# Attention of nine pairs in 64-token sub-chunks on 64x64 tiles, with r loaded four tokens to a partition and w spread by a product

## The chip, the cores and the metric

The kernel runs on one core of a Trainium2 chip. The metric is the device time of one execution in microseconds; the median of several runs counts. A core has a matrix engine (TensorE, PE in the profile; its weight loads are PEld), a vector engine (VectorE, DVE), a scalar engine (ScalarE, ACT), a general engine (GpSimd, POOL) and a queue engine for transfers (SyncE, SP). They run side by side, each through its own instructions in order, and wait for each other by semaphores. Sixteen DMA engines move data between the device memory and the on-chip memory of 128 partitions. TensorE writes to eight banks of 128 x 512 float32.

## The reference

Four batches, eight heads, 768 tokens, 48 channels a head. First a decaying linear attention, then a block that mixes tokens and channels:

```python
def _attn_ref(r, k, v, w, u):
    state = np.zeros((B, H, D, D))
    for t in range(S):
        kt, vt, rt = k[:, :, t], v[:, :, t], r[:, :, t]
        cur = np.einsum('bhd,bhe->bhde', u[None] * kt, vt)
        y[:, :, t] = np.einsum('bhd,bhde->bhe', rt, state + cur)
        state = w[None, :, :, None] * state + np.einsum('bhd,bhe->bhde', kt, vt)

def _moe_ref(x, w_theta, w_tok_r, w_tok_i, w_ch):   # x: y with heads side by side
    theta = x @ w_theta
    zr, zi = x * np.cos(theta), x * np.sin(theta)
    u = x + (np.einsum('ts,bsd->btd', w_tok_r, zr) + np.einsum('ts,bsd->btd', w_tok_i, zi))
    return u + np.maximum(u @ w_ch, 0.0)
```

## The kernel before

The 768 tokens of a batch are three *pairs* of 128-token chunks, so there are twelve pairs, g = 0 to 11 (g = 3b + pr). `front(b)` does attention, theta and z for the three pairs of a batch, `mixing(b)` the token and channel products. In a pair, k and r are multiplied by powers of w (`kpow`, `rpow`; tasks Kw and Rw, DVE or POOL, L539 and L541), transposed by TensorE against the identity (`flip`, L477) and copied out of the bank (L492 on ACT, L493 on DVE) to KT and RT. Then come the scores K'R (L585), their causal mask (mAT, L594, always on DVE), the diagonal with the bonus u (PD L601, diag L618, yd L627), the outer products of k and v for the state (L651), the running state (sums F and T, L695 to L703; decay N, L706; 16-bit copies Sb or Sd, L666 to L685) and the output, as states times r plus masked scores times v, gathered in two banks y.

There are two forms of a pair. In the *two-token form* (pairs 0 to 6, those in `PAIRS`) a partition holds two neighbouring tokens, k and v come in pieces of 384 bytes, scores are 64x64 tiles with 128 columns, four masks of 512 columns are made, the states' product (L727), two straight products (L740) and the bonus (L756) add up in the banks, and ACT or DVE copies x out (L764, L766). In the *chunk form* (pairs 7 to 11) k and v come in pieces of 192 bytes, scores are 64x128 tiles by rows (16 products), there are four masks too, the states take 16 products of 64 rows (L779), the masked scores times v 16 full products (L792), and DVE adds yd while it takes x out (L801). r always comes with two tokens to a partition.

x is transposed, by TensorE or by a DMA (L483), and multiplied by w_theta (L815); ACT takes cosine and sine (L822, L826), DVE makes z (L830). In `mixing`, six products of 128 tokens sum over z (`mix`, L852: for each of six output chunks three parts of four products), DVE adds x (un, L870), then comes a transpose, the product with w_ch (L884), and the last sum: DVE alone (L893), or ACT and POOL (L890, L897). The token weights are cast to 16 bits by POOL's transfers (`cast`, L446), transposed by TensorE in twelve blocks (`weights`), and used by the mixing from then on.

The powers of w: `w_row` is loaded by ACT's queue into all 128 partitions (L293), in a part of the memory of z; ACT takes its logarithm (L374) and six exponentials scaled by token counts (L381).

Nothing of the order is left to a scheduler on the chip. Each piece of work is a *task*; lists written out by hand give the order of all tasks (`ORDER`), the engine where there is a choice (`WAYS`), the bank of each use (`BANKS`), extra waits (`AFTER`) and filler products of zeros that write to an idle bank (`IDLE`, and the tasks warm0 and warm1 of six and eight products; all at L284). Each engine executes its tasks in that order and waits where an operand isn't there yet.

## Time and profile before

| | |
|---|---|
| median of 3 runs | 139.91 us (139.69 to 140.66) |
| profiled execution, first to last instruction | 138.9 us |
| PE, DVE, ACT, POOL busy | 127.6, 107.5, 76.7, 61.7 us |
| q1 (SP's and ACT's transfers): packets, share of 16 DMA engines | 64720, 75.6% |
| q0 (POOL's casting loads): packets, share | 2432, 12.4% |
| loads of k and v, chunk form | 20 of 192 KB |
| loads of k, v (two-token form) and r | 7, 7 and 12 of 384 KB |

The profile gives one time for its execution, the span, and the three times of the runs apart from it; the median of the runs is 1.0 us above the span. Busy time counts the time in which an engine has an instruction in work; for PE the ends of instructions are modelled, and neighbouring ones overlap, so that the length of one is more than its share of a row of them. Where a line lists a wait, the name behind the arrow is what ended it.

### The profile page before, as it was taken

The numbers are of one execution on the slowest core, as the hardware profiler recorded it, in microseconds if no ns is written. First come the engines' busy times: TensorE is split into PE (matmuls) and PEld (weight loads), VectorE is DVE, ScalarE is ACT, GpSimd is POOL, SyncE is SP. The second block draws the span as 40 slices with busy tenths as digits, with TensorE's granted clock in tenths as the row PEclk, the third lists the DMA queues.
The fourth block names the chain that finished last, engine by engine and source line by source line (L and its number), as shares of the span: only waits on it lengthen the run. The fifth ranks groups of instructions, "written<-read, shape, count | busy, mean of one in ns | idle before, by whom it ended". The sixth has DMA issues, their size and how long they took to land.

```text
span 138.9 us, 4469 instructions
## 1 busy us (share of the span) xinstructions
PE 127.6 (92%) x1874; PEld 85.0 (61%) x1874; DVE 107.5 (77%) x205; ACT 76.7 (55%) x145; POOL 61.7 (44%) x70
## 2 busy tenths in 40 slices
PE   0999569999996999999999999999999999999990
PEld 0334347977764767777766687577565665656640
DVE  2419397889799999999979997999699986427281
ACT  2455687799992368593898039629903133650020
POOL 5003977861041099949320199993118902002000
PEclk9999985799999999999999999999999999999999
DMA  2999999999999999739979999999972563803635
GB/s 46 250 263 263 261 225 213 210 239 211 248 254 267 261 196 147 107 67 174 193 127 267 169 217 185 147 269 187 288 177 60 103 181 87 257 0 115 114 122 218
DMA packets 67340, 25.65 MB, mean 185 GB/s; under 512 B 61816, under 2 KB 67320, under 8 KB 67320
## 3 DMA queue, kind: packets, MB, share of 16 engines
q1 hardware_dynamic: 64720, 22.22, 75.6%
q0 software_dynamic: 2432, 2.95, 12.4%
q10 hardware_dynamic: 168, 0.20, 0.7%
q8 instruction: 14, 0.23, 0.7%
q14 instruction: 6, 0.05, 0.1%
HBM read 20.25 MB, written 4.72 MB: 180 GB/s over the span
## 4 chain that ended last, share of the span: by engine, by line
PE 65%; DVE 10%; DMA 8%; POOL 6%; SPq 4%; issue 2%; ACT 2%; DVEq 0%; ACTq 0%; POOLq 0%
PE bank L852 25%; PE bank L477 9%; DMA ld<-in_v_dram 8%; PE bank L815 6%; PE bank L884 5%; PE bank L284 5%; PE bank L585 4%; POOL Kw L539 3%; PE bank L651 2%; SPq L432 2%; PE bank L740 2%; DVE Rw L539 2%; DVE PD L601 2%; PE bank L756 1%; PE bank L792 1%
## 5 line engine op out<-in xcount | busy, mean ns | idle before, releaser
L852 PE MATMUL bank<-z,WrT 128*128 128x384 bf16 x144 | 46.8, 326 | 0.0
L852 PE MATMUL bank<-z,WiT 128*128 128x384 bf16 x144 | 46.8, 326 | 0.0
L594 DVE TENSOR_TENSOR mAT<-bank,mask 128x512 bf16<-128x512 f32 x28 | 18.1, 681 | 4.3 <-PE bank L585 4.1
L539 POOL TENSOR_TENSOR Kw<-ld,kpow 128x768 bf16<-128x768 f32 x4 | 8.2, 2040 | 24.5 <-DVE Kw L539 9.9
L852 PEld LDWEIGHTS <-WrT 128*128 128x128 bf16 x144 | 14.0, 98 | 8.1
L852 PEld LDWEIGHTS <-WiT 128*128 128x128 bf16 x144 | 14.1, 98 | 8.0
L870 DVE TENSOR_TENSOR uu_all<-bank,x 128x384 bf16<-128x384 f32 x24 | 13.0, 549 | 4.9 <-PE bank L852 4.7
L826 ACT ACTIVATE trig<-bank 128x384 f16<-128x384 f32 x24 | 11.4, 504 | 7.9 <-PE bank L815 7.8
L627 POOL TENSOR_TENSOR yd<-dg,vb 128x768 bf16<-128x768 f32 x10 | 14.7, 1470 | 2.3 <-ACT lwu L403 1.3
L492 ACT ACTIVATE RT<-bank 128x1024 bf16<-128x1024 bf16 x11 | 11.3, 1026 | 6.8 <-PE bank L477 6.6
L884 PE MATMUL bank<-Wch,uu_all 128*128 128x384 bf16 x72 | 14.6, 326 | 0.1
L897 POOL TENSOR_TENSOR fin_all<-fin_all,uu_all 128x384 f32<-128x384 f32 x8 | 7.3, 913 | 16.1 <-ACT fin_all L890 14.8
L815 PE MATMUL bank<-Wth,xT 128*128 128x384 bf16 x72 | 14.3, 326 | 0.0
L284 PE MATMUL bank<-zero 128*128 128x512 bf16 x31 | 10.9, 503 | 3.6 <-DVE zero L291 3.6
L822 ACT ACTIVATE trig<-bank,pi 128x384 f16<-128x384 f32 x24 | 13.6, 594 | 0.7 <-PE bank L815 0.6
L830 DVE TENSOR_TENSOR z<-x,trig 128x1536 bf16<-128x1536 bf16 x12 | 11.7, 974 | 2.9 <-ACT trig L822 2.9
L492 ACT ACTIVATE KT<-bank 128x1024 bf16<-128x1024 bf16 x11 | 11.5, 1044 | 3.3 <-PE bank L477 3.0
L594 DVE TENSOR_TENSOR mAT<-bank,mask_c 128x512 bf16<-128x512 f32 x20 | 13.0, 681 | 0.2 <-PE bank L585 0.2
L539 POOL TENSOR_TENSOR Rw<-ld,rpow 128x768 bf16<-128x768 f32 x4 | 7.2, 1812 | 8.2 <-DVE PD L601 8.1
L893 DVE SCALAR_TENSOR_TENSOR fin_all<-bank,uu_all 128x384 f32<-128x384 f32 x16 | 8.6, 551 | 2.2 <-PE bank L884 1.8
L539 DVE TENSOR_TENSOR Rw<-ld,rpow 128x768 bf16<-128x768 f32 x8 | 9.2, 1152 | 1.0 <-DMA ld<-in_r_dram 1.0
L477 PE MATMUL bank<-ident,Kw 128*128 128x128 bf16 x96 | 7.4, 219 | 2.5 <-POOL Kw L539 2.5
(112 smaller groups left out, 219.6 us busy)
## 6 DMA issues: line engine op xcount, KB each, us to landing
ld<-in_r_dram SPq DMA_DIRECT2D x12, 384.0 KB, 6.0
out_dram<-fin_all SPq DMA_DIRECT2D x11, 384.0 KB, 3.1
ld<-in_k_dram SPq DMA_DIRECT2D x7, 384.0 KB, 10.5
ld<-in_v_dram SPq DMA_DIRECT2D x7, 384.0 KB, 6.1
ld<-in_k_dram SPq DMA_DIRECT2D x10, 192.0 KB, 4.8
ld<-in_v_dram SPq DMA_DIRECT2D x10, 192.0 KB, 5.2
z<-in_moe_w_tok_i_dram POOLq DMA_DIRECT2D x1, 384.0 KB, 7.3
fin_all<-in_moe_w_tok_r_dram POOLq DMA_DIRECT2D x1, 384.0 KB, 8.4
```

The costliest lines, as they stand in the source:

```text
L284: ins = [nc.tensor.matmul(bank_t[k][:, :wide * C].rearrange("p (a c) -> p a c", a=wide), zero, bc(zero, 1, wide), start=True, stop=True, s ...
L477: ins = [nc.tensor.matmul(bank16(tok)[:, i * C:(i + 1) * C], s, ident, is_transpose=True, start=(i == 0), stop=(i == n - 1)) for i, s in e ...
L492: ways = [act(n * C, lambda: nc.scalar.activation(dst, src(), Act.Copy)), dve(n * C, lambda: nc.vector.tensor_copy(dst, src()), 1.0 if pai ...
L539: return eng.tensor_mul(to.rearrange("p j h d -> p h j d")[:, :, :, :D], tokens(i), pw)
L594: mask01[:, j] if pairs else mask_c): nc.vector.tensor_mul(
L627: return eng.tensor_mul(yd.rearrange("p a b d -> p (a b) d"), wide(dg, D), vb.rearrange("p a b d -> p (a b) d"))
L815: ins = [nc.tensor.matmul(bank(th)[:, :HD], xT[:, t, dk, :], Wth[:, dk, :], start=(dk == 0), stop=(dk == ND - 1)) for dk in range(ND)]
L822: P.add(act(HD, lambda th=th, t=t, trig=trig: nc.scalar.activation(trig[:, t, 0], bank(th)[:, :HD], Act.Sin, bias=pi2), 144), use=[th], rd ...
L830: P.add(dve(4 * HD, lambda trig=trig, pr=pr: nc.vector.tensor_mul(z[:, 2 * pr:2 * pr + 2], bc(x[:, 2 * pr:2 * pr + 2], 2, 2), trig), 2.0, ...
L852: ins.append(nc.tensor.matmul(bank(tm)[:, :HD], (WrT, WiT)[ri][:, so, to * C:(to + 1) * C], z[:, so, ri], start=(part == 0 and i == 0), st ...
L870: P.add(dve(HD, lambda tm=tm, t=t, to=to, un=un: nc.vector.tensor_add(un[:, t], bank(tm)[:, :HD], x[:, to])), use=[tm], rd=[("x", xi, pr, ...
L884: ins = [nc.tensor.matmul(bank(tf)[:, :HD], uT[:, t, dk, :], Wch[:, dk, :], start=(dk == 0), stop=(dk == ND - 1)) for dk in range(ND)]
```

## The change

Pairs 3 to 11, nine in all, get a new form; pairs 0 to 2 keep the two-token form.

- In the new form k and v lie as in the chunk form. Each 128-token chunk is two sub-chunks of 64 tokens. The scores are 32 products of 64x64 tiles with 64 columns, only the two diagonal blocks of a chunk, so that a pair has two masks of 512 columns in place of four. The state is carried from sub-chunk to sub-chunk: three sums F (or two and a last Sb) and up to four 16-bit states in place of two. The states take 32 products in two tasks, the masked scores times v 32, the outer products 32 on 64x64 tiles. The second mask waits for the states' second task (`fence`).
- r is loaded with four neighbouring tokens of a head to a partition, in pieces of 768 bytes, by two DMAs of 64 partitions each. `rpow` has four exponentials of 192 columns, and the transposes of r give the heads in the order 0, 2, 1, 3 of the head pairs.
- w is loaded as one row; ACT takes its logarithm on one partition, TensorE multiplies it by a column of ones into two banks (`spread`), and the exponentials read the banks.
- `wu`, the small load for w and u by channel, may go by POOL's queue or SP's too; sums, casts and copies get other engines.
- Order, engines, banks, extra waits and fillers are new throughout. POOL issues the first casting load before its first Kw, four behind that Kw, one after Kw1, and the one for w_theta after Kw2; all twelve weight transposes stand before the first mixing product in PE's order. PE's order begins: spread, wu flip, K flip of pair 0, a weight flip, the eight fillers warm1, outer products of pair 0, r flip of pair 0, scores. DVE's order from the first Rw to the first z is Rw0, vb0, mask, KT copy, F, a weight copy, PD0, wup, Rw1, place, two masks, blank, uw, T, Sb, yd0, three masks, PD1, two masks, a weight copy, a mask, two weight copies, an x copy, mask_c, Sb, F, a weight copy, T, Rw3, Rw2, N, z0. The last sums are on DVE alone 21 times (16 before), on ACT and POOL 3 times (8 before).

The core of the diff:

```diff
-PAIRS = (0, 1, 2, 3, 4, 5, 6)
+PAIRS = (0, 1, 2)
...
 IDLE = [
-    (28, 0, 5), (73, 3, 5), (71, 3, 5), (83, 2, 1), (119, 0, 1),
+    (21, 2, 2), (32, 3, 3), (5, 5, 3), (91, 7, 1), (81, 7, 1), (88, 3, 2), (99, 0, 3),
+    (100, 5, 3), (44, 4, 2), (135, 1, 1), (166, 3, 2),
 ]
...
-        P.add((ACT, 2950, False, lambda: nc.scalar.dma_start(out=w_row, in_=rows_of(w, C))),
-              wr=["w_row"], prio=-3e4, name="w_row", kind="small")
+        P.add((ACT, 460, False, lambda: nc.scalar.dma_start(
+            out=w_row, in_=w.rearrange("(a h) d -> a h d", a=1))),
+              wr=["w_row"], prio=-3e4, name="w_row", kind="small", desc=(2, 1, 70))
...
+        def spread():
+            ins = [nc.tensor.matmul(bank("lw")[:, :HD], ones, w_row.rearrange(
+                "p h d -> p (h d)"), start=True, stop=True, skip_group_check=True)]
+            for hh in range(2):
+                ins.append(nc.tensor.matmul(
+                    bank("lw4")[hh * Q:(hh + 1) * Q, :HD // 2], ones[:, :Q],
+                    w_row[:, hh * HP:(hh + 1) * HP].rearrange("p h d -> p (h d)"),
+                    start=True, stop=True, skip_group_check=True))
+            return ins[0], ins[-1]
+        P.add(pe(1900, spread), rd=["lw", "ones"], acq=["lw", "lw4"], prio=-199.5, mode=5,
+              name="spread")
...
+        if what == "r":
+            for hh in range(2):
+                P.add(sp(lambda hh=hh: nc.sync.dma_start(
+                    out=Ls[i][hh * Q:(hh + 1) * Q].rearrange("p (x n) -> p x n", x=HP),
+                    in_=rows[hh * HP:(hh + 1) * HP].rearrange("x (p i) d -> p x (i d)", i=4))),
+                    wr=[("L", i, hh)], prio=-90 + 0.001 * nload[0], desc=(0, 16, 38.5),
+                    name="load r", kind="load")
...
+                def fine(tk=tk, KT=KT, RT=RT):
+                    ins = []
+                    for c in range(2):
+                        for y in range(HP):
+                            for hi, a in ((0, 0), (1, 1), (0, 1), (1, 0)):
+                                q, s = slice(hi * Dp, (hi + 1) * Dp), slice(a * Q, (a + 1) * Q)
+                                o = (c * HP + y) * Q
+                                ins.append(nc.tensor.matmul(
+                                    bank(tk[hi])[s, o:o + Q], KT[q, y, c, s], RT[q, y, c, s],
+                                    start=(c == 0 and y == 0), stop=(c == 1 and y == HP - 1),
+                                    skip_group_check=True))
+                    return ins[0], ins[-1]
...
+                        ins.append(nc.tensor.matmul(
+                            bank(ts[a])[hi * Dp:(hi + 1) * Dp, o:o + D], Kw[q, m, h, :], vm,
+                            start=first, stop=(hp == HP - 1), skip_group_check=True))
...
+            steps = [(ts[0], 0)] if pairs else [(ts[0], 0), (ts[1], 0), (ts[0], HP * D)]
+            for n, (tok, o) in enumerate(steps):
+                S, kS = new_sb(pairs)
+                Ss.append((S, kS))
...
+                add_up(F, tok, o, [kF], running)
+                to_16(S, kS, pairs, F, kF, "Sb1")
+                running = (F, kF)
...
+                def states(ty=ty, RT=RT, Ss=Ss, c=0, begun=begun):
+                    ins = []
+                    for y, hp in enumerate(at_slot):
+                        for hi, a in ((0, 0), (1, 1), (0, 1), (1, 0)):
+                            S = Ss[2 * c + a][0]
+                            if S is None:
+                                continue
+                            q, s = slice(hi * Dp, (hi + 1) * Dp), slice(a * Q, (a + 1) * Q)
+                            o = (c * HP + hp) * D
+                            ins.append(nc.tensor.matmul(
+                                bank(ty[hi])[s, o:o + D], RT[q, y, c, s], S[q, hp, :],
+                                start=(hi, a) not in begun, stop=False, skip_group_check=True))
+                            begun.add((hi, a))
+                    return ins[0], ins[-1]
...
+                masked(0)
+                masked(1, held, [("states", g)])
+
+                def intra(ty=ty, vb=vb, m=mAT2[0], off=0):
+                    m = m.rearrange("p i h t -> p i (h t)").rearrange(
+                        "p i (x t) -> p i x t", t=Q)
                     ins = []
                     for c in range(2):
                         for hp in range(HP):
-                            for hi in range(2):
...
+                            for a in range(2):
+                                s, hi = slice(a * Q, (a + 1) * Q), a ^ off
                                 o = (c * HP + hp) * D
                                 ins.append(nc.tensor.matmul(
...
+                                    bank(ty[hi])[s, o:o + D],
+                                    m[s, hi, c * HP + at_slot[hp], :],
+                                    vb[s, c, 2 * hp + hi, :], start=False,
+                                    stop=(c == 1 and hp == HP - 1), skip_group_check=True))
```

398 lines of the change are left out of this document (205 added, 193 removed), and 83 rows, old and new, of the table ORDER.

## The prediction

> **What bounds the kernel now.** I read the page's shares and slices first, then busy time by stretch, then the chain of waits, then single rows of the start. The first fence has lines of the page: span, busy share of two engines, granted TensorE clock and DMA share in 40 slices of 3.47 us.
>
> ```profile
> span 138.9 us, 4469 instructions
> PE 127.6 (92%) x1874; PEld 85.0 (61%) x1874; DVE 107.5 (77%) x205; ACT 76.7 (55%) x145; POOL 61.7 (44%) x70
> ...
> PEclk9999985799999999999999999999999999999999
> DMA  2999999999999999739979999999972563803635
> ```
>
> The second fence is the busy time of each engine by stretch; the numbers in brackets are instructions.
>
> ```profile
> 9.50:18.50 9.00, 6.44 (x82) 3.67 (x82) 6.00 (x14) 5.25 (x6) 5.94 (x5) 1.00 1.26 263
> ...
> 19.80:26.30 6.50, 6.50 (x133) 4.84 (x133) 5.49 (x11) 4.87 (x13) 4.22 (x7) 0.50 1.19 211
> ...
> 43.00:66.00 23.00, 23.00 (x530) 16.76 (x532) 22.62 (x43) 12.81 (x25) 15.04 (x17) 1.00 0.94 169
> 66.00:115.00 49.00, 48.69 (x673) 33.37 (x670) 43.99 (x77) 27.20 (x53) 25.25 (x23) 1.00 0.93 183
> 115.00:131.00 16.00, 16.00 (x100) 9.67 (x99) 6.90 (x11) 4.99 (x11) 1.82 (x2) 1.00 0.50 123
> ```
>
> From 43 us on PE is busy in all but 0.3 us of 88 us, so there the time is the sum of PE's work. DVE is nearly full beside it until 66 (22.62 of 23.00) and has room later (6.90 of 16.00). Before 43 PE is fed badly: the DMA engines are full, DVE is busy for two thirds (6.00 of 9.00) to five sixths (5.49 of 6.50) of the time, and from 19.8 to 26.3 TensorE has half its clock. So two numbers decide: when the first mixing product starts (the first work that PE has in plenty), and how much PE work is left then. The third fence has pieces of the chain in order of time (start, length, what).
>
> ```profile
> 35.50 0.65 PE bank L852 x4
> ...
> 37.57 0.68 PE bank L477 x12
> ...
> 40.37 2.50 DVE Rw L539
> 42.87 0.05 issue
> ...
> 60.16 0.34 PE bank L727 x8
> 60.50 0.50 PE bank L740 x32
> 61.00 0.34 PE bank L756 x4
> 61.35 0.57 PE bank L585 x32
> 61.92 0.76 PE bank L651 x48
> ...
> 80.86 0.55 PE bank L585 x16
> 81.42 0.32 PE bank L779 x16
> ...
> 84.69 0.40 PE bank L792 x16
> ...
> 86.18 0.24 PE bank L651 x8
> ...
> 134.58 0.68 PE bank L884 x3
> ```
>
> The first mixing product starts at 35.5, the last PE work ends at 135.3 (134.58 + 0.68): 99.8 us, in which PE once waits about 1.1 us, for the slow decay product at 40.37 that ends at 42.87. After 135.3 come 3.6 us of last output. 35.5 + 99.8 + 3.6 = 138.9, the span. The median of the runs is 139.9, so 1.0 us lies around the span; I add it at the end.
>
> **PE's work behind the first mixing product.** (a) The attention forms. A pair in the old two-token form costs, from these pieces, states 0.34, straight products 0.50, bonus 0.34, scores 0.57, outer products 32/48 of 0.76 = 0.51: 2.26 us, without transposes and the diagonal, which all forms share. A pair in the old chunk form: scores 0.55, states 0.32, products with v 0.40, outer products 2 x 0.24 = 0.48: 1.75. The new form issues four groups of 32 products on 64x64 tiles. Its groups exist in the trace only as relatives: 32 products cost 0.50 (48 columns, two row tiles), 0.51 (48 columns, four tiles) and 0.57 (128 columns, four tiles). I take 0.50 each and 0.1 more because the states are split into two tasks between other work: 2.10. Four pairs (3 to 6) leave the two-token form, 4 x -0.16 = -0.6; five (7 to 11) leave the chunk form, 5 x 0.35 = +1.75: +1.1 in all. Bounds: if a group costs two thirds of that (0.34, as 8 wide products do), 9 x -0.64 brings the +1.1 to -4.7; if 32 small products cost twice what 16 do (0.80), 9 x 1.2 brings it to +12. The three relatives lie at 0.50 to 0.57, so I stay near them. Half the masks and fewer columns go away, but not PE instructions: their number doubles against the chunk form. (b) The new order puts all twelve weight transposes ahead of the first mixing product; before, six lay behind it. 36 products at 0.68/12 = 0.057 are -2.0. (c) In return all of pair 2's attention comes behind it, 2.26 less half its outer products, which the last pair of a batch doesn't need: +2.0, and one x transpose more, +0.34. Sum: +1.1 - 2.0 + 2.0 + 0.3 = +1.4. (d) The 1.1 us wait at 42: in the new order that place looks different, and I take the wait as gone; if its like returns, that is +1.1.
>
> In a sentence by itself: the Trainium skill, "TensorEngine Tiling (Array Packing)", section Key Properties, says that a change of tiling mode drains TensorE; the new PE order changes mode 53 times where the old did 44, and this trace agrees in kind, since 16 states cost 0.32 and 32 products 0.50 with changes around them. By that rule alone the sum would be about 1 us longer, by 9 changes at an estimated 0.1 us; the split states above hold nearly all of it already.
>
> **The start.** The fourth fence has rows of the start in order of time.
>
> ```profile
> 2.45 1.28 ACT L303 ACT_TABLE_LOAD   x1 [2.45 <-issue]
> ...
> 5.55 0.52 ACT L374 ACTIVATE z<-z 128x384 f32<-128x384 f32 x1 [1.82 <-DMA z<-in_w_dram]
> ...
> 6.63 1.10 ACT L381 ACTIVATE rpow<-z,tok_f 128x384 f32<-128x384 f32 x2
> ...
> 9.85 0.96 DVE L539 TENSOR_TENSOR Rw<-ld,rpow 128x768 bf16<-128x768 f32 x1
> ```
>
> The logarithm of w waits 1.82 us for w in 128 rows. As one row it should come sooner; the bounds are the end of the table load, 3.73, and 5.55. I take 4.1, near the lower, for 1.5 KB is little. Then 0.52 for the logarithm; then the new product that spreads the row, whose price no row shows: the change plans 1.9 us for three products, the first of which is half the columns, 0.95 (from below 0.3, if it ran as the 512-column fillers do; from above 1.9). Then four full exponentials at 0.55, four half as wide at about 0.35 (192 columns) and a small one of 0.2, in ACT's queue before the last rpow: 3.8. The first r decay starts at 4.1 + 0.52 + 0.95 + 3.8 = 9.4, against 9.85: little gained, since twice as many exponentials stand in its way.
>
> From there DVE's own queue up to the first z (which releases the first mixing product) is the bound, since PE has slack there (it is given 23 filler products). The fifth fence has the groups that price it: mean ns of one stands after the comma.
>
> ```profile
> L594 DVE TENSOR_TENSOR mAT<-bank,mask 128x512 bf16<-128x512 f32 x28 | 18.1, 681 | 4.3 <-PE bank L585 4.1
> ...
> L830 DVE TENSOR_TENSOR z<-x,trig 128x1536 bf16<-128x1536 bf16 x12 | 11.7, 974 | 2.9 <-ACT trig L822 2.9
> ...
> L601 DVE TENSOR_TENSOR PD<-RT,KT 128x1024 bf16<-128x1024 bf16 x10 | 7.2, 720 | 0.3 <-ACT RT L492 0.3
> ...
> L801 DVE TENSOR_TENSOR x<-bank,yd 128x384 bf16<-128x384 f32 x10 | 5.2, 551 | 1.6 <-PE bank L792 1.5
> ...
> L493 DVE COPY WrT<-bank 128x768 bf16<-128x768 bf16 x4 | 2.2, 545 | 0.0
> ...
> L699 DVE TENSOR_TENSOR F<-bank,N 128x192 f32<-128x192 f32 x4 | 1.4, 354 | 0.3
> ```
>
> 8 masks x 0.681 = 5.4; 4 Rw x 0.95 = 3.8; 6 copies of transposes x 0.545 = 3.3; 2 PD x 0.72 = 1.4; z 0.97; five sums of 192 x 0.354 = 1.8; yd0 about 0.95 (as a decay product). That is 17.6. The K copy, v's cast, two state casts and the small constants that stand among them I estimate at 5.0 from rows of like size. 22.6 in all, plus 1.0 for the first F, which waits until PE is through eight fillers and the first outer product: 9.4 + 22.6 + 1.0 = 33.0, and 0.2 to the product. First mixing product at 33.2, against 35.5. Before, the same place was reached with four masks more done, but the half clock cost PE time there; now PE has the weight transposes to fill it, so a half clock would cost less.
>
> DVE in all: masks 18 x -0.681 = -12.3; 18 more sums x 0.354 = +6.4; five more x and five more final sums at 0.55 = +5.5; four K and four x transposes copied on DVE instead of one each, about +3.6; fewer Kw, PD, casts, about -2. Sum +1.2: DVE is not relieved, its masks are traded for work that ACT and POOL had. Behind the first mixing product its share remains as it was, so it costs nothing more than now; if its cover were gone, each us of DVE before 66 would be a us. Where the second mask waits for the states (the new fence), DVE's queue behind it waits too; this is up to 9 short waits, and I allow them to be hidden.
>
> **DMA.** The sixth fence compares loads in 0 to 12 us with 19 to 36 us, when POOL's casting loads of the weights run.
>
> ```profile
> ld<-in_r_dram SPq DMA_DIRECT2D x3, 384.0 KB, 5.9
> ```
>
> ```profile
> q0 software_dynamic: 1936, 2.51, 82.8%
> q1 hardware_dynamic: 2933, 1.11, 32.6%
> ...
> ld<-in_r_dram SPq DMA_DIRECT2D x2, 384.0 KB, 13.7
> ```
>
> While casts run (q0), SP's loads get 1.11 MB in 17 us, 65 GB/s, and land 13.7 us after issue instead of 5.9. The casts are moved forward: one ahead of POOL's first Kw, four right behind it. r in 768-byte pieces gains a little, k and v of pairs 3 to 6 in 192-byte pieces lose a little; I take these as equal, for the DMA engines are full until about 55 us (the slices) either way and the loads come in the order of their use.
>
> **The sum.** 33.2 + (99.8 - 1.1 + 1.4) + 3.6 = 136.9 for the span; the 0.2 that the fence waits may show makes it 137.1, and with the 1.0 around it 138.1 (-1.3%).
>
> **The rivals.** *Slower, starved start:* five casts before 16 us take the DMA engines for about 14 us (six took 17), in which SP gets 65 x 14 = 0.9 MB. Pair 1's second half of r must be in DVE's hands at about 15.4 (9.4 and the 6 us that stand before Rw1); all behind it, masks of pair 0 too, waits in order. If it lands at 20 the first mixing product comes at 37.8 and the time is 142.7; it is slower by over 1% from a landing at 18.6. Against it: r1 and k1 are issued early, and some will have landed before the casts start. In a sentence by itself: the Trainium skill, "DMA: Bandwidth & Descriptors", section Queues, rings and completion order, says that an engine turns between queues by whole packets, so a queue of large packets gets the larger part; the 82.8% against 32.6% above agree.
> *No change:* the small products cost 0.57 instead of 0.50 a group, or fence waits show: 9 x 0.28 = 2.5 more, 140.6.
> *More:* the groups cost 0.40 and the start holds: 9 x -0.4 = -3.6, 134.5; half of it 136.3.
>
> **How the numbers follow.** Forecast (137.0 to 139.2) 0.42; more (below 137.0) 0.20; no change by dearer products (139.2 to 141.3) 0.16; starved start (above 141.3) 0.22. One per cent, 1.4 us, is about what a measurement of this kernel can tell from no change. Faster by over 1% (below 138.5): 0.20 and 0.27 of the forecast, 0.47. Within: 0.15 + 0.16 = 0.31. Slower: 0.22. The range 135.5 to 142.6 leaves out about a tenth on each side; the forecast's own is 137.0 to 139.2.
>
> **What would show it.** Right: the first L852-like mixing product near 33, PE without gaps from about 35 on, groups of 32 products near 0.50, masks 30 instead of 48. Wrong: Rw1 on DVE waiting for a load, PE idle before 20 for longer than now, a late theta product waiting for its weight, or DVE full and PE with gaps between 40 and 110.

## The result, and the profile after

| | before | changed |
|---|---|---|
| median | 139.91 us | 155.51 us (153.76 to 155.88) |
| ratio | | 1.106 (95% interval 1.099 to 1.114) |
| span of the profiled execution | 138.9 us | 153.5 us |
| first mixing product starts | 35.34 | 39.11 |
| last PE work ends | 135.24 | 149.50 |

The change made the kernel 15.6 us slower. Medians are over all executions; the ratios, here and below, leave out those that ran in a slower state of the chip. In the prediction the first mixing product before is at 35.5, since the chain shows its second piece; it starts at 35.34. The first fence has lines of the changed kernel's page, to be laid beside those of before.

```profile
span 153.5 us, 5331 instructions
...
PE 133.3 (87%) x2286; PEld 86.8 (57%) x2286; DVE 108.4 (71%) x223; ACT 72.4 (47%) x146; POOL 58.8 (38%) x62
...
PEclk9999999999999999599999999987999999999999
DMA  1999999999999999858778999999999396611545
...
L660 DVE TENSOR_TENSOR mAT<-bank,mask_c 128x512 bf16<-128x512 f32 x18 | 11.8, 683 | 1.2 <-PE bank L856 0.7
```

PE has 2286 products in place of 1874, but is busy only 5.7 longer. The span grew by 14.6, so most of it is time in which PE did nothing. (The medians lie 15.6 apart. In nearly all executions recorded later the time is 1.7 to 1.9 above the span, so the 138.9 must belong to the slowest of the three runs before, 140.66.) Recorded half clock stood in slices 6 to 8 before, where PE had slack; now it stands in the 17th and in the 27th and 28th, where PE has none. The clock row is no witness for the start: the trace's clock records begin at 17.05 (at 9.29 before), and until then PE worked at about half its later speed, as the fillers below show. The DMA engines are full from the second slice on, as before; the hole of before in slices 17, 18 and 21 is one from 17 to 22 now. The next two fences, of before and after, give the stretch from the first mixing product to the last PE work (length, busy time of PE, PEld, DVE, ACT and POOL, granted clock, DMA share, GB/s).

```profile
35.34:135.24 99.90, 98.40 (x1395) 66.59 (x1392) 83.97 (x143) 53.08 (x103) 44.19 (x42) 1.00 0.84 172
```

```profile
39.11:149.50 110.39, 103.17 (x1871) 68.54 (x1867) 84.57 (x159) 52.47 (x110) 43.32 (x37) 0.97 0.90 155
```

The ledger of the 14.6 follows from them: 3.8 in the start (39.11 - 35.34), 4.8 more of PE's busy time (103.17 - 98.40), 5.7 more of PE's idle time (7.22 - 1.50), and 0.4 in the tail. The waits of PE in that stretch, from the view of waits, are these (what PE's line waited for: sum, times, longest):

```profile
PE bank L524 <- POOL Kw L592: 2.2, 1, 2.2
PE bank L718 <- issue: 1.9, 1, 1.9
PE bank L973 <- DMA uu_all<-uu_all: 1.5, 1, 1.5
PE bank L524 <- DVE uu_all L959: 1.1, 1, 1.1
PE bank L973 <- DVE x L891: 0.3, 1, 0.3
```

Before, that view has one line there, the 1.1 for Rw that the prediction named. The first is pair 10's K, whose load landed at 100.3; the second is a wait "for nothing that the profile shows"; the third a DMA transpose that took 4.96; the fourth a transpose of K on PE behind work of DVE, which had itself waited 1.59 and 0.41 for loads of r and k (from 85.8 on). The start is in these rows of DVE and PE:

```profile
12.40 0.96 DVE L587 TENSOR_TENSOR Rw<-ld,rpow 128x768 bf16<-128x768 f32 x1 [8.67 <-DMA ld<-in_r_dram]
...
17.85 0.36 DVE L750 COPY F<-bank 128x192 f32<-128x192 f32 x1 [2.50 <-PE bank L718]
```

```profile
12.77 4.66 PE L292 MATMUL bank<-zero 128*128 128x512 bf16 x11
17.36 0.44 PE L718 MATMUL bank<-vb,Kw 64*64 64x48 bf16 x32
...
25.42 2.10 PE L292 MATMUL bank<-zero 128*128 128x512 bf16 x9
```

The exponentials were ready at 9.35, but Rw0 waits for the second half of r until 12.40. Eleven fillers stand ahead of the outer products and take 4.66, 0.42 each, where nine of them take 2.10 later, 0.23 each; F waits for the outer products until 17.85.

### The profile page after: what moved, and what is told of

It is laid out like the page before. It is cut to its first block, busy times and chain, and to the rows that moved or that the text cites. A ratio compares the mean times of both kernels' runs of the same rounds, so it can differ in the third digit from the quotient of the medians.

```text
span 153.5 us, 5331 instructions
## 1 busy us (share of the span) xinstructions
PE 133.3 (87%) x2286; PEld 86.8 (57%) x2286; DVE 108.4 (71%) x223; ACT 72.4 (47%) x146; POOL 58.8 (38%) x62
## 3 DMA queue, kind: packets, MB, share of 16 engines
q1 hardware_dynamic: 67100, 22.23, 80.8%
## 4 chain that ended last, share of the span: by engine, by line
PE 64%; DMA 10%; DVE 7%; ACT 7%; issue 4%; POOL 3%; SPq 2%; DVEq 0%; ACTq 0%; POOLq 0%
PE bank L941 24%; PE bank L973 9%; PE bank L524 9%; DMA ld<-in_k_dram 7%; PE bank L292 6%; PE bank L905 5%; DMA uu_all<-uu_all 3%; PE bank L881 2%; PE bank L648 2%; ACT WrT L539 1%; DVE mAT L660 1%; PE bank L718 1%; PE bank L856 1%; SPq L476 1%; POOL Kw L590 1%
## 5 line engine op out<-in xcount | busy, mean ns | idle before, releaser
L973 PE MATMUL bank<-Wch,uu_all 128*128 128x384 bf16 x72 | 15.7, 350 | 1.9 <-DMA uu_all<-uu_all 1.5
L697 POOL TENSOR_TENSOR yd<-dg,vb 128x768 bf16<-128x768 f32 x10 | 14.6, 1473 | 6.3 <-DVE pi L306 5.2
L959 DVE TENSOR_TENSOR uu_all<-bank,x 128x384 bf16<-128x384 f32 x24 | 12.7, 551 | 5.5 <-PE bank L941 5.3
L982 DVE SCALAR_TENSOR_TENSOR fin_all<-bank,uu_all 128x384 f32<-128x384 f32 x21 | 11.2, 553 | 5.7 <-PE bank L973 5.7
L587 DVE TENSOR_TENSOR Rw<-ld,rpow 128x768 bf16<-128x768 f32 x8 | 7.9, 992 | 10.3 <-DMA ld<-in_r_dram 10.3
L292 PE MATMUL bank<-zero 128*128 128x512 bf16 x37 | 13.0, 481 | 0.0
L524 PE MATMUL bank<-ident,Kw 128*128 128x128 bf16 x96 | 8.1, 233 | 5.6 <-POOL Kw L590 2.3
L660 DVE TENSOR_TENSOR mAT<-bank,mask_c 128x512 bf16<-128x512 f32 x18 | 11.8, 683 | 1.2 <-PE bank L856 0.7
L524 PEld LDWEIGHTS <-Kw 128*128 128x128 bf16 x96 | 6.6, 104 | 8.3 <-POOL Kw L590 3.2
L973 PEld LDWEIGHTS <-uu_all 128*128 128x128 bf16 x72 | 6.9, 106 | 6.5 <-DMA uu_all<-uu_all 2.0
L539 ACT ACTIVATE KT<-bank 128x1024 bf16<-128x1024 bf16 x8 | 8.2, 1030 | 4.9 <-PE bank L524 4.9
L891 DVE TENSOR_TENSOR x<-bank,yd 128x384 bf16<-128x384 f32 x18 | 9.2, 550 | 0.5 <-POOL N L781 0.3
```

The costliest lines, as they stand in the source:

```text
L292: ins = [nc.tensor.matmul(bank_t[k][:, :wide * C].rearrange("p (a c) -> p a c", a=wide), zero, bc(zero, 1, wide), start=True, stop=True, s ...
L524: ins = [nc.tensor.matmul(bank16(tok)[:, i * C:(i + 1) * C], s, ident, is_transpose=True, start=(i == 0), stop=(i == n - 1)) for i, s in e ...
L539: ways = [act(n * C, lambda: nc.scalar.activation(dst, src(), Act.Copy)), dve(n * C, lambda: nc.vector.tensor_copy(dst, src()), 1.0 if pai ...
L587: return eng.tensor_mul(to.rearrange("p i x d -> p x i d")[:, :, :, :D], fours(i), pw)
L660: mask01[:, j] if pairs else mask_c): nc.vector.tensor_mul(
L697: return eng.tensor_mul(yd.rearrange("p a b d -> p (a b) d"), wide(dg, D), vb.rearrange("p a b d -> p (a b) d"))
```

## The experiments

Four theories were set against each other. (1) The new order costs: late loads, products and fillers ahead of pair 0, stores and transposes ahead of loads in SP's queue. (2) The new form of nine pairs costs. (3) The new load formats slow the DMA. (4) PE waits for its own instructions. All edits are to the changed kernel's lists, unless said otherwise; in diffs a line gives an engine's order. There r0a and r0b are the two halves of pair 0's load of r (k and v alike), wu is the small load of w and u, `cast Wi2` a casting load and `flip Wi5` a transpose on PE of a token weight's block, TU a transpose of an output block by DMA, `out` an output store, and a number behind "fillers" their count. The first four runs have line numbers 7 lower than the changed kernel.

**The start, step by step.**

```diff
-SP: wu w, r0b, k0, v0, r0a, ...
+SP: r0b, r0a, k0, wu w, v0, ...          (first run)
-POOL: cast Wi2, Kw0, cast Wi1, ...
+POOL: Kw0, cast Wi2, cast Wi1, ...       (second run, with the first)
-WARM = [6, 8]; 3 fillers behind warm1
+WARM = [6, 1]; none behind warm1         (third run, with both)
```

> Changed kernel; in SP's order the loads of r (pair 0, both halves) and of k (pair 0) come before the small load of w by channel. Nothing else is moved. Changed kernel: median 155.5, Rw0 begins at 12.40 after a wait for r's second half, first mixing product at 39.23. If the late first loads set the start (theory 1): Rw0 begins at 10.0 to 11.0, the first mixing product comes 1 to 2.4 earlier, total 153.0 to 154.5. If the new form of nine pairs is what costs (theory 2): no gain beyond 0.5. If DMA as a whole is slower by the new formats (theory 3): r's loads get shorter waits only as far as others get longer ones, total within 0.5 of 155.5.

> As the run before, and the first casting load, of a token weight, is issued behind Kw0 instead of before it on POOL. Theory 1 (the casting load takes DMA share from r, k and v of pair 0): Rw0 begins at 9.4 to 10.0, which is when the last of its exponentials is there, first mixing product at 36 to 37.5, total 152 to 153.5. Theory 2: no gain. If the casting load doesn't matter: the same as the run before within 0.3.

> As the run before, and ten of the eleven filler products ahead of pair 0's outer products are left out (warm1 one product in place of eight, the three behind the weight flip gone). Theory 1: the outer products begin when Kw0 and vb0 are there, so F of pair 0 comes 2 to 3 earlier than in the run before, but the granted clock may stay at 0.5 longer; first mixing product 1 to 3 earlier than in the run before if the clock doesn't matter, equal or later if the fillers had bought the clock. Theory 2: no gain.

Measured: 154.32, 155.59 and 154.57; first mixing product at 40.3, 42.8 and 41.1. In the first Rw0 came at 11.82, as the late load of w now held up ACT's exponentials. Rw0 did come at 9.4 in the second and third, just as the prediction had it, and nothing was won: PE's fourth task is the flip of a weight block, and it now waited for its casting load. This is PE in the second run:

```profile
9.16 1.03 PE L517 MATMUL bank<-ident,Kw 128*128 128x128 bf16 x8 [0.18 <-POOL Kw L583]
16.81 0.39 PE L517 MATMUL bank<-ident,z 128*128 128x128 bf16 x2 [6.62 <-DMA z<-in_moe_w_tok_i_dram]
```

Between the first and the second run only that casting load was moved, and Rw0 came 2.4 earlier (9.40 for 11.82): the casting load had held up the loads beside it. With it moved, the weight came late in its place. All of theory 1's numbers for the first mixing product were missed; its total for the first run (153.0 to 154.5) was met, but with a later start, so not for its reason.

**The new form in the old order.**

```diff
-order of the changed kernel
+order of the kernel before, mapped task by task; PAIRS = (0, 1, 2)
```

> The new form of nine pairs, with all loads in their new formats and the spread of w, but tasks in the order of the kernel before: its order on all engines, the masked scores of a new-form pair held back by three PE tasks behind its states, no extra waits by hand, five groups of fillers as before. Only where the new form uses more banks at a time are some tasks of pairs 9 and 10 later. Theory 1 (the new order and its queues cost, the form doesn't): first mixing product at 33 to 36, total 138 to 143. Theory 2 (the form costs): first mixing product as in the kernel before, total 150 or more, the difference spread over pairs 3 to 11. Theory 3 (the load formats cost): loads of k and v land late, PE waits on Kw and Kw's DMA from pair 5 on, total 147 or more.

Measured: 156.51, ratio 1.114 (1.104 to 1.124), first mixing product at 37.5. This hits theory 2's number, but not its reason: PE had gaps of 10.9 behind the first mixing product. Of these, 4.4 lay between 114 and 120, where PE's outer products and others waited for DVE's sums F and T; whether a lack of banks was behind that is tested in the fourteenth run, below.

**Start and loads.** The fifth run also moves what stood ahead of pair 0 on PE and DVE. The sixth changes SP's order in the middle only, and the eighth does both.

```diff
-PE: wuflip, flip K0, flip Wi5, warm1 x8 +3, outer0, flip R0, scores0.1, flip K1, scores0.0, flip Wi2
+PE: wuflip, warm1 x3, flip K0, flip R0, outer0, scores0.1, flip K1, scores0.0, flip Wi5, flip Wi2
-SP: v6a, out2, k7b, k7a, out1, r9a, TU0, k9b, r9b, k9a, v7b, out0, ...
+SP: v6a, k7b, k7a, k9b, k9a, r9a, r9b, out2, out1, TU0, v7b, k10b, k10a, out0, ...
```

> Changed kernel with four edits to the start, nothing else: r and k of pair 0 first in SP's order and the first casting load behind Kw0 (as in the second run); warm1 three products in place of eight and ahead of pair 0's K flip, the three more fillers behind it gone; r's flip ahead of the outer products; the flip and the copy of the first weight block, for which PE waited 6.0 in the second run, moved behind the scores on PE and behind the masks on DVE. Theory 1 (the start is lost by the order of DMAs, and by products that stand ahead of pair 0 in PE's order): Rw0 at 9.4, F of pair 0 at about 12, first mixing product at 33 to 36 (39.1 before the edits), total 149.5 to 152. If the start is bound by DMA as a whole (rival: 4.6 MB land by 25): the weight flips wait for their casts, first mixing product at 38 or later, total 154 or more.

> Changed kernel with SP's order alone changed in its middle: the loads of k for pairs 7 and 9, and of r for pair 9, ahead of the first two output stores, k of pair 10 ahead of the third, k of pair 11 ahead of the transposes by DMA of x for pair 6. Theory 1 (the late loads of k stand behind stores and transposes that wait for DVE): the gaps of 1.06 at 90.6 and of 2.21 at 100 in PE go, and with the second the half clock at 102 (1.7); total 151 to 153. Theory 3 (DMA is full, so loads land late whatever their order): the gaps move to others of the same size, total within 1 of 155.5. The gap of 1.87 at 59.4 stays in both.

> The edits of the fifth and of the sixth run together. Theory 1: their gains add up, as they are in different stretches: total 146 to 149. Theory 2 (the new form costs): neither gains, 154 or more. If one bottleneck (DMA) is behind both: the sum of the gains is halved.

Measured: 153.58 (1.094, 1.087 to 1.101), 154.35 (1.104, 1.096 to 1.112) and 155.47 (1.106, 1.098 to 1.113); first mixing product at 38.8, 39.1 and 38.1. The gains don't add up, and by the intervals that of the sixth run can't be told from none. The fifth run's start is the one that the rival named (38 or later), its total is in neither range; the sixth run's total is in neither either, and the eighth's is in that of theory 2. In the sixth run the waits of 2.2 and 1.1 behind loads are gone, and others stand in their place:

```profile
PE bank L973 <- DMA uu_all<-uu_all: 3.0, 2, 2.3
PE bank L718 <- issue: 2.2, 1, 2.2
```

PE waits 3.0 for transposes in place of 1.5. The transpose of 72 us took 5.53 from issue to landing in place of 4.96, now with more loads issued beside it; that this is why is likely, not shown. So PE's idle time did not fall (7.4 for 7.2). What the sixth run gained is busy time, 101.46 for 103.17, with one window of half clock in place of two. In the eighth run, once PE was early, DVE stood still. These rows are of DVE and POOL:

```profile
12.65 4.66 DVE L671 TENSOR_TENSOR PD<-RT,KT 128x1024 bf16<-128x1024 bf16 x1
```

```profile
12.40 1.83 POOL L590 TENSOR_TENSOR Kw<-ld,kpow 128x768 bf16<-128x768 f32 x1
14.15 0.76 POOL L493 DMA_DIRECT2D x<-in_moe_w_tok_i_dram  x1
14.93 1.82 POOL L590 TENSOR_TENSOR Kw<-ld,kpow 128x768 bf16<-128x768 f32 x1
```

PD takes 0.69 in the changed kernel's start; here it ends 0.6 after POOL's second Kw (in the fifth run it took 4.31 in the same place).

**PE's own instructions.**

```diff
-                unread(k, n, 4)
+                unread(k, 4 * n, 1)
```

> Changed kernel with each filler product of 512 columns cut into four of 128: the same time on PE, but 198 more products and weight loads ahead of pair 3. The gap of 1.87 at 59.4 was recorded ahead of PE's 1729th instruction in the changed kernel and in the first two runs, and in the third too, where 20 fewer instructions stand before it and the products there are others; 1729 and 3521, where a further gap was recorded twice, are seven times 256 apart. If the gap is PE's wait for its instructions (theory 4): no gap of over 1 at the products where it was; if there is one, it is at instruction 1729 or another one that differs from it by a multiple of 256. If it comes of the work itself: the gap stays at the same products. Total 153.5 to 156 in either case.

Measured: 156.67, a little above the 153.5 to 156 expected. The three fences are PE around the gap in the changed kernel, in the third run (ten fillers fewer ahead of it), and in this one.

```profile
59.02 0.43 PE L718 MATMUL bank<-vb,Kw 64*64 64x48 bf16 x30
61.32 0.21 PE L718 MATMUL bank<-vb,Kw 64*64 64x48 bf16 x2 [1.87 <-issue]
```

```profile
60.87 0.44 PE L711 MATMUL bank<-vb,Kw 64*64 64x48 bf16 x32
61.12 0.31 PE L874 MATMUL bank<-vb,mAT 64*64 64x48 bf16 x8
62.76 0.30 PE L874 MATMUL bank<-vb,mAT 64*64 64x48 bf16 x8 [1.33 <-issue]
```

```profile
60.79 0.41 PE L881 MATMUL bank<-vb,mAT 64*64 64x48 bf16 x15
63.34 0.18 PE L881 MATMUL bank<-vb,mAT 64*64 64x48 bf16 x1 [2.14 <-issue]
```

With ten fillers fewer the gap comes exactly ten products later (the two left of the outer products and eight of the next group): it belongs to a place in PE's stream of instructions, not to an operation. Counted in the trace over all of PE's records in order of start, it stands behind number 1729 in the changed kernel and in the first, second, third, fifth, sixth and eighth run too, and behind 1985 = 1729 + 256 in this one, where a new gap of 0.79 appears behind 961 = 1729 - 3 x 256. The page has the transfers that bring the instructions, 16 KB each:

```profile
q8 instruction: 18, 0.29, 0.8%
```

So theory 4 holds for this gap: it comes at places 256 instructions apart, whatever the work there. In these eight kernels PE used up the 256 instructions ahead of it in 2.4 to 2.7 (groups of 32 small products are 64 instructions in about 0.4), and 4.0 to 5.0 had passed since the first of them when it went on. Before, the blocks around that place took 4.1 to 7.1, and no gap is recorded. But 4.0 to 5.0 is no general limit: in the changed kernel itself the block that ends at number 3521 was used up in 2.4 without a gap, and in the second run, in 2.2, with one of 0.7. How far ahead the instructions were at either place, no view shows. The Trainium skill, "Runtime: NRT & Kernel Launch", section Instruction fetch mechanics, also has refills of 256 instructions, and calls their cost mostly hidden; here it was not hidden: the gaps of these eight kernels at number 1729 or 1985 were 1.3 to 2.2.

**Both ends again, and the clock.** The tenth run gives the start another order (Kw1 on DVE, Kw2 behind the casts, pair 1's scores ahead of the weight flips, eight fillers in all); the eleventh adds to the sixth a transpose by PE instead of a DMA and two tasks with few instructions between the small products; the twelfth has both.

```diff
-SP: TU0                      -PE: scores5.0, intra3.0, outer4, intra3.1, mix0.1.2, flip R7
+PE: flip TU0; ACT: out TU0   +PE: mix0.1.2, scores5.0, intra3.0, flip R7, outer4, intra3.1
```

> Changed kernel with the start put in another order (beyond the fifth run): Kw1 on DVE in place of POOL, and Kw2 behind all casts on POOL, since in the fifth and eighth runs PD of pair 0 took 4.66 on DVE while POOL worked on Kw1 and Kw2 (0.69 otherwise); mask and place ahead of Rw0; KT of pair 0 copied by ACT; the weight flips of the first blocks behind pair 1's scores; seven fillers in place of 22 or so in front of the first mixing product. Theory 1 (the start is a matter of order): PD of pair 0 begins at 13 and takes 0.7, first mixing product at 33 to 36 (38.8 in the fifth run), total 149 to 152. If DVE's work ahead of z0 or the weights' casts set it whatever the order: first mixing product at 37 or later.

> Changed kernel with the loads as in the sixth run, and two edits more behind pair 3: the transpose of the first output block of batch 0 by PE and ACT in place of a DMA, and a mixing part and a flip of r moved between the products of 64 by 64 of pairs 3 to 5. Theory 1: the gap of 2.26 at 75.3 of the sixth run falls to 0.5 or less, as nothing waits for a transpose there any more. Theory 4 (PE can't have more than 256 instructions in 4.0 to 4.6 us, as the times between its 1473rd and its stalled 1729th instruction show): 1.25 us more of work with few instructions stands between, so the gap of 2.25 at 60.4 falls to 0.5 to 1.2. Total 150.5 to 152.5.

> The edits of the two runs before together. Theory 1 (waits that the order makes, and the half clock after them, are the whole loss; the form of nine pairs is not): 143 to 147. Theory 2: 150 or more.

Measured: 155.14, 155.53 and 154.17. All three totals miss theory 1's ranges, the tenth's start is the rival's (37 or later), and the twelfth's total is in theory 2's range. In the tenth and twelfth PD begins at 12.7 and 12.5 and takes 0.7, as expected; in the eleventh and twelfth the transpose's wait at 75 goes and the instruction gap shrinks (to 1.2 and 0.7). But the first mixing product is at 38.2 in the tenth and 37.8 in the twelfth, where PE works at half clock from 17.1 to 27.3. The thirteenth puts fillers back where PE waited, 31 in all, and has three transposes (TU0 as in the twelfth, TU3, TU4) on PE in place of DMA.

```diff
-WARM = [1, 2]; fillers: spread 2, wuflip 3
+WARM = [4, 2]; fillers: spread 2, wuflip 3, outer0 4, diag0 3, flip K1 8, flip R1 5
```

> The twelfth run with three edits: fillers back at the start, 31 in all, each group put where PE waited in the twelfth run (behind the outer products, the diagonal, K's and r's flips of pair 1); r's flip of pair 1 and the weight flips in another order, so that they do not wait for banks; the transposes of three output blocks of batch 0 and 1 (the first, fourth and fifth) by PE and a copy in place of DMAs. If the half clock at the start (10.2 of it in the twelfth run) comes of PE's idle time there: no half clock before the first mixing product or at most 3.4, and it comes at 33.5 to 36 (37.8). If half clock comes whatever PE does: 37.5 or later. The gap of 1.35 at 100.6, a wait for a transpose by DMA, goes, if that DMA was its cause. Total by theory 1: 147.5 to 151.

Measured: 151.73, ratio 1.079 (1.073 to 1.085). Half clock at the start fell from 10.2 to 3.4: the fillers that were taken away had bought the clock. There is none behind the first mixing product, and PE's idle time there fell to 4.4 (7.2 in the twelfth run). The first mixing product did not come earlier, 38.45, so the half clock was not what set it; ahead of it PE waits 2.46 for a weight's casting load.

**What sets the first mixing product.** The sixteenth run puts pair 1's scores and pair 0's output ahead of the weight flips (and leaves out two fillers of warm0), the seventeenth theta and z of pair 0 as well, the eighteenth two casting loads and four flips behind.

```diff
-PE: flip R1, states0, flip Wi4, Wr4, Wi3, Wi2, Wi5, scores1.0, straight0.0, ...
+PE: flip R1, scores1.0, states0, straight0, bonus0, scores1.1, diag1, flip Wi5, Wi4, Wi2, Wi3, Wr4
-POOL: cast Wi2, Wi1, Wr2, Wr1, Wr0, Wi0, Wth     (16)
+POOL: cast Wi2, Wr2, Wi1, Wr1, Wth, Wr0, Wi0     (18)
```

> The thirteenth run with the start in one more order: pair 1's scores and pair 0's output ahead of the weight flips on PE (in the thirteenth run PE waited 2.46 at 19.87 for a weight's casting load, and DVE, with pair 0 done at 21.2, waited 5.75 for pair 1's scores behind those flips). If that order sets the first mixing product: 33 to 36 (38.45), total 146.5 to 149.5. If the casting loads or the twelve weight flips themselves set it (they land or stand ahead of the mixing whatever the order): within 1 of 38.45, total 150.5 or more.

> The run before with theta and z of pair 0 ahead as well: x's flip of pair 0 ahead of the second token weight's flips on PE, theta's products behind two of them, cosine and sine between the weights' copies on ACT, z0 ahead of Rw3 and Rw2 on DVE. z0 then has 2 of other DVE work less before it. If z0 sets the first mixing product: 1.5 to 3 earlier than in the run before, total 145 to 148. If the weights' flips and copies do: no gain over the run before beyond 0.5.

> The sixteenth run (first mixing product at 36.56; PE waited there 1.18 at 25.6 and 1.10 at 28.3 for casting loads of token weights and 1.08 at 30.6 for that of w_theta) with two of the six casting loads of token weights put behind w_theta's, and the four weight flips that need them moved behind the first mixing products on PE. If the landing of the casting loads sets the start (the rival of a starved start): first mixing product at 33 to 35, and the three waits go or halve; the stretch behind it becomes 2.0 longer by the four flips, so the total changes by 1 at most: 149.5 to 151.5 beside 151.0. If something else sets it: 36 or later, total 152 or more.

Measured: 151.02 (1.079, 1.071 to 1.087) with the first mixing product at 36.56, between the two ranges expected; 153.82 (1.093, 1.084 to 1.102) with it at 42.3, as theta now waited 3.17 for its weight, so that this run decides nothing; and 34.85 in the eighteenth, whose six times (median 154.89) lie too far apart, 149.9 to 157.7, to judge its total. The sixteenth run's PE shows three waits for casting loads:

```profile
26.74 0.51 PE L524 MATMUL bank<-ident,z 128*128 128x128 bf16 x6 [1.18 <-DMA z<-in_moe_w_tok_r_dram]
29.35 0.84 PE L524 MATMUL bank<-ident,x 128*128 128x128 bf16 x12 [1.10 <-DMA x<-in_moe_w_tok_i_dram]
31.65 1.76 PE L905 MATMUL bank<-Wth,xT 128*128 128x384 bf16 x5 [1.08 <-DMA Wth<-in_moe_w_theta_dram]
```

In the eighteenth the view of waits from 20 to 34.8 has none for a casting load, but others in their place:

```profile
PE bank L802 <- ACT Sd L739: 1.9, 2, 1.4
PE bank L524 <- ACT KT L539: 0.8, 1, 0.8
PE bank L718 <- ACT WrT L539: 0.5, 1, 0.5
```

So 3.4 of waits went and the first mixing product came 1.7 earlier. That run also took four flips, 24 products or 1.4 by the prediction's 0.057, from ahead of it. The 1.7 may be no more than these, so it is not shown that the casting loads set the start; they are one wait of several, and the next one stood behind it.

**The form once more, in the old order.** The fourteenth run mends the fourth: banks, and the flip of w and u behind five fillers. The fifteenth has the new form on pairs 7 to 11 only; the ninth was the same without the mends.

```diff
-PE: ..., mix2.0.1, outer11, outer9, outer10, mix2.3.0, ...
+PE: ..., outer9, mix2.0.1, outer10, mix2.1.0, mix2.1.1, mix2.3.0, ..., intra9.1, outer11, ...
-PAIRS = (0, 1, 2)
+PAIRS = (0, 1, 2, 3, 4, 5, 6)     (9 and 15)
```

> The code of the changed kernel with the two-token form for pairs 0 to 6, as in the kernel before, in the order of the kernel before: the new form stands only where the chunk form stood (pairs 7 to 11); r by four tokens and w by the product as in the change. The run with the new form on nine pairs in this order had the first mixing product at 37.5, gaps of 10.7 behind it, and 156.5. If the new form on pairs 3 to 6 cost there (it puts more work on DVE's sums than this order left room for, and more instructions on PE): 143 to 148, few gaps between 43 and 75. If the new form costs wherever it stands: gaps behind 103 stay, 148 to 152. If the loads of r or the product for w cost: first mixing product at 37 or later as before, and 152 or more.

> The new form of nine pairs in the order of the kernel before, as in the fourth run, with two mends: the outer products of pairs 9 to 11 stand where banks are free for them (in the fourth run they came late, and PE had gaps of 4.3 between 114 and 120 with 6.8 of half clock), and the flip of w and u stands behind five fillers in place of 14, its copy on DVE behind Rw0. If the lack of banks, which the new form's order makes, was the cause there: gaps behind 110 under 1.5, no half clock there, and Rw0 at 9.4: total 147 to 150.5. If the new form's waits arise anyway: 153 or more.

> As the run before with the two-token form for pairs 0 to 6, so that the new form stands only where the chunk form stood. If each pair of the new form costs alike: 143 to 147, the kernel before plus five ninths of the loss of the run before. If the new form costs only among pairs 3 to 6, where two-token pairs stood before: 140 to 143. If the loads of r and the product for w cost most: the same as the run before within 1.

Measured: 156.94 (1.111, 1.104 to 1.118) for the ninth, 151.97 (1.080, 1.074 to 1.086) for the fourteenth, and 149.28 (1.054, 1.046 to 1.062) for the fifteenth. The ninth, with its first mixing product at 37.6, fits the branch of r's loads and the product for w; the fourteenth and fifteenth lie in none of their ranges. The two mends were worth 4.5 in the fourteenth against the fourth run: the half clock behind 110 is gone there, and of the waits one of 1.5 is left, so a lack of banks is a likely cause of that part. By the ratios the kernel with the form on nine pairs is 11.2 above the one before, with the form on five 7.6, so 3.6 more on four further pairs (2 to 5, given the intervals). The fifteenth loads k and v as the kernel before does, so their new format is not its reason; the new form of five pairs, r's format and w's product stay together in the 7.6. This is its stretch from the first mixing product to the last PE work:

```profile
36.75:144.19 107.44, 101.54 (x1715) 67.30 (x1712) 82.55 (x143) 55.44 (x109) 48.09 (x46) 1.00 0.87 157
```

Beside the kernel before that is 1.4 later in the start, 3.1 more of busy time at full clock and 4.4 more of idle time; most of its waits are for DVE.

## Why the prediction was wrong, point by point

The forecast was 138.1, in a range of 135.5 to 142.6; 155.5 was measured, 17.4 more. In the terms of its sum, 5.9 of that are the start (39.1 for 33.2), 10.1 the stretch from the first mixing product to the last PE work (110.4 for 100.3), 0.4 the tail, and 1.0 what lies around the span (2.0 for 1.0, see above).

- **PE's work behind the first mixing product (+1.4): a near size, in part by luck.** At full clock throughout, PE is busy for 100.24 (second run) and 100.68 (fifth run) there, which is 1.8 to 2.3 above before:

```profile
38.82:147.03 108.21, 100.68 (x1870) 66.51 (x1867) 84.81 (x159) 52.44 (x110) 43.34 (x37) 1.00 0.90 153
```

  The terms behind it were off and cancel. A group of 32 small products costs less than the 0.50 taken, by the changed kernel's chain, which refutes the rival of dearer products:

```profile
94.22 0.38 PE bank L648 x32
94.60 0.47 PE bank L856 x32
```

  Counted in the trace, each product up to the start of the next, the four groups of a new pair take 1.7 in the fifth run (2.10 taken), and the nine pairs 14.6 in place of 15.7 before: term (a) is about -1.1, not +1.1. Against that, six products of theta more lie behind the first mixing product (66 for 60, which the sum left out), +1.4 by that count, and the same mixing and w_ch products take 1.8 more, perhaps because the last one ahead of a wait counts at its full length. The 0.32 and 0.50 that the prediction gave for a drain at a change of tile form show no price of one, and no run does.
- **Step (d), and the 0.2 for waits: failed, 5.7 of idle time.** The prediction took the one wait of before as gone and allowed nearly nothing in its place. The signs that the text named for being wrong, gaps of PE between 40 and 110, came. They are of several makes: late loads of k and r, a transpose by DMA, a stall at the end of a block of 256 instructions. Taking one away let others appear: PE's idle time stayed at 7.2 to 7.4 in the sixth and twelfth run, and fell only with the thirteenth and sixteenth, to 4.4 and 4.6.
- **The clock: not in the sum.** Two windows of half clock, 3.41 each, are recorded right behind the two longest gaps (from 61.42 and 102.38). PE's busy time is 2.5 to 2.9 more than at full clock (103.17 against 100.24 and 100.68). The prediction spoke of the half clock in the start only. The Trainium skill, "TensorE: Matmul & The Clock Gate", section What's actually happening, has a window of 3413 ns and half clock after an idle one; the 3.41 agree, but gaps of 1.9 and 2.2 were enough here. At the start it allowed 1.0 for the first F's wait behind fillers and outer products; the eleven fillers alone took 4.66, at half their later speed.
- **The start (33.2): failed, 39.1.** The step that failed is that DVE's own queue up to the first z would be the bound, with one wait of 1.0 in it. This is the changed kernel from Rw0 to the end of z0:

```profile
12.40:39.06 26.66, 23.97 (x398) 15.71 (x396) 20.64 (x45) 14.70 (x26) 9.58 (x10) 1.00 1.16 214
```

  DVE's work was even less than priced, 20.6 in place of 22.6. But its queue began 3.0 late (12.40 for 9.4), since r was not there, and it stood still for 6.0 (26.66 - 20.64) in place of 1.0: 2.5 for the first F behind PE's slow fillers, 2.5 for ACT (RT's copy, the diagonal, cosine and sine), and the rest for scores and outer products. 3.0 - 2.0 + 5.0 is the 6.0 by which z0 ended late (39.06 for 33.0). The 9.4 for the exponentials was met, 9.35, but by two errors that cancel: the logarithm began at 3.36 in place of 4.1, and the product for w with the waits around it took 1.74 (from 3.88 to 5.62) in place of 0.95. Rw0 at 9.4 was measured in ten of the runs, those in which r came earlier.

  The rival of a starved start was given 0.22. Its kind of cause was right: a casting load put ahead held up the loads beside it. Its place was wrong, for pair 0's Rw waited, not pair 1's, and once that was mended the weight flips on PE did. Its 37.8 for the first mixing product was nearer than the forecast (39.1), and its 142.7 for the whole far off, since it had none of the waits behind.
- **DMA taken as equal: not so in sum.** In the medians of the trace it was: pieces of 192 bytes took 15 ns, of 384 bytes 26 (before), of 768 bytes 49 (changed), which is 2.0 more for k and v and 1.2 less for r, spread over 16 engines. But the pages' shares say otherwise:

```profile
q1 hardware_dynamic: 64720, 22.22, 75.6%
```

```profile
q1 hardware_dynamic: 67100, 22.23, 80.8%
```

  75.6% of 138.9 is 105.0, and 80.8% of 153.5 is 124.0: for the same bytes each engine spent 19 us more, of which the medians explain 0.8. The mean packet took longer, of 192 bytes 20.1 ns for 17.4, of 256 bytes (transposes) 32.9 for 27.4. Whether that is a cause of the late loads or comes of other transfers running side by side is open. A run with the old formats alone was not made, so theory 3 is not excluded; the fifteenth run speaks only against the new format of k and v as the reason for its own loss.
- **DVE (+1.2): right.** It is busy for 108.4 against 107.5, with 30 masks (18 of them in the page's line above) in place of 48.

What stays open. The best orders found for the nine pairs, the thirteenth and sixteenth run, both stand at 1.079 in place of 1.106: 11 slower than the kernel before. The sixteenth's profiled execution, 147.1, was its fastest, and is 8.2 above the profile of before: 1.2 in the start, 3.8 in PE's busy time, 3.1 in idle time (1.0 of the 3.8 are the three transposes that went to PE, 18 products by the prediction's 0.057). No single cause was found for the rest. Theory 2, that the form itself costs, is not excluded: the form on five pairs alone, in the old order, was 7.6 slower, and DVE, for which PE waits most there, is the place to look next. That another order would close the gap is neither shown nor excluded, and no version beat the kernel before.

```profile
36.56:143.39 106.83, 102.23 (x1889) 68.04 (x1886) 85.17 (x159) 55.28 (x113) 43.12 (x37) 1.00 0.89 154
```

## What to carry to other kernels

A sum of PE's work is only as good as the waits left out of it: where every engine's order is fixed by hand and the DMA is nearly full, a new order should be priced by asking of each load and transpose when it can land, before content is counted. Waits taken away one at a time gave back little, as the next stood behind (in the sixth run 3.3 of waits behind loads gone, idle time the same, 1.2 gained by the clock); such a change is judged by its ledger of start, busy time, idle time and clock. A form with twice as many, half as large instructions can also run out of instructions where its groups stand close together, as at number 1729 here; with other work put between them that stall was smaller (1.2 and 0.7 in the eleventh and twelfth run).

## What the hardware showed that was not expected

- PE stalled for no other visible reason at places that lie multiples of 256 apart in its stream: 1.3 to 2.2 at number 1729 (1985 in the seventh run) where 256 instructions had been used up in 2.4 to 2.7, 0.8 at 961, and 0.5 to 1.6 at 3521 in four runs. Fast blocks did not always stall (2.4 at 3521 in the changed kernel).
- Operations of DVE took far longer while POOL worked on a Kw that had begun before them, and ended 0.6 to 0.8 behind it: PD took 4.66 instead of 0.69 beside two Kw, and in the thirteenth run Rw took 2.58 instead of 0.96 beside a Kw of 1.86.

```profile
14.16 2.58 DVE L587 TENSOR_TENSOR Rw<-ld,rpow 128x768 bf16<-128x768 f32 x1
```

- Fillers cost time where work waits behind them and earn it where they keep the clock: with 8 of them in place of 37 the start had 10.2 of recorded half clock (twelfth run), with 31 put into PE's waits 3.4 (thirteenth).
